# First loads of a gated two-branch mixer: their queues and order, a dummy gelu, and the count of products on zeros

## The chip, the cores and the metric

The kernel runs on one core of a Trainium2 chip. The metric is the device time of one execution in microseconds, as the median of several runs. A profile of one execution gives a span (from the first instruction of the program to its last) and that execution's own time, which is a little longer.

The engines are named as in the profile: PE (TensorE, matrix products; PEld its weight loads), DVE (VectorE), ACT (ScalarE), POOL (GpSimd) and SP (SyncE, which here only issues transfers). Transfers are issued by SP or by ACT, each on a queue of its own, and carried out by 16 DMA engines that both share.

## The reference

One sequence of 2048 tokens with 512 features goes through two branches, which a gate mixes. All tensors are bf16.

```python
x = A_x
g = _sigmoid((x * gate_w).sum(-1, keepdims=True))
a = _A_ref(x, A_wqkv, A_w_phi, A_wo)        # linear attention, 32 heads of 16
b = _B_ref(x, B_w_in, B_w_sp, B_b_sp, B_w_out)
return g * a + (1 - g) * b
```

Branch B is where the kernel starts:

```python
z = _gelu(jnp.einsum('bsd,df->bsf', x, w_in))    # w_in is 512 x 1376
z1 = z[..., :Fh].copy()
z2 = _layernorm(z[..., Fh:], axis=-1)
g = jnp.einsum('ts,bsf->btf', w_sp, z2) + b_sp[None, :, None]   # w_sp is 2048 x 2048
return jnp.einsum('bsf,fd->bsd', z1 * g, w_out)
```

Branch A projects x to q, k and v, applies a small matrix per head and a softmax of both signs to q and k, sums k times v over the sequence, and divides.

## The kernel before

The 2048 tokens are cut into 16 tiles of 128. The order of the instructions on each engine is written out by hand. The work goes in stages: z for every tile (with the projection of v and the folding of the heads' small matrix into the weights of q and k mixed in), then k's features beside the product with w_sp, then q's features, the rest of that product and the output tiles.

The change touches the opening alone. The names in it:

- `xn` (lines 109 and 112) holds the first two tiles of x as they lie in memory. `x_transpose(t)` (line 186) multiplies each with the identity matrix on PE, four products of 128x128, and two casts on DVE (line 195) write the result to `xT`, the transposed x that all projections read. The columns of `xT` for the other tiles come from transposing loads on SP (lines 116 and 122).
- `w_in` holds the weights of z in four blocks of 128 rows. It is loaded in pieces: columns 0 to 511 in two halves of two row blocks each (lines 110 and 111), columns 512 to 1023 (line 113) and columns 1024 to 1375 (line 115). Its last column, number 1376, is not loaded: `gate_column()` (line 197) puts gate_w there, so that the gate's sum comes out with z.
- `gw` (line 114) is gate_w as four rows, 1 KB.
- `z_piece(t, n0, n1)` (line 170) is four products (one per row block) for one tile and one of three column pieces, on line 173; `z_gelu` (line 203) is the gelu on ACT that reads the result. `z_post` (line 208) also writes `gth`, the tanh of the gate's sum, one column per tile.
- `spin(n)` (line 180) is n products of 128x128 on `warm`, a tile of zeros, whose result nobody reads.

The opening on PE runs in the order of lines 452 to 466: products on zeros, the transposition of tile 0, two more on zeros, the first piece of z for tile 0, the transposition of tile 1, the gate column, three on zeros, then the other pieces of z for tiles 0 and 1. Each step waits for the loads and casts that it reads. The cast into the gate column (line 201) waits for both halves of the first piece of w_in and for the third piece.

The issues of SP and ACT stand in lines 109 to 151; on SP each goes out when the one before it is done issuing. ACT loads its table for gelu ahead of the first gelu. Each later load on SP, from line 117 on, also waits for a load eight places earlier in the order of issue.

Of the kernel before, what the change touches and what calls it, by code (L numbers as in the profile page):

```python
# [7 lines left out]
AF = mybir.ActivationFunctionType  # L8
# [6 lines left out]
P = 128  # L15
# [4 lines left out]
F = 1376  # L20
# [4 lines left out]
CH = 512  # L25
# [14 lines left out]
def kernel(  # L40
# [14 lines left out]
    nc = tc.nc  # L55
    x2 = A_x.flatten_outer_dims()
# [10 lines left out]
    def zbank(t):  # L67
# [4 lines left out]
    w_in = pers.tile([P, NDT, F + 1], BF16, name="w_in")  # L72
# [16 lines left out]
    xn = pers.tile([P, 2, D], BF16, name="xn")  # L89
    warm = pers.tile([P, P], BF16, name="warm")  # L90
# [4 lines left out]
    gth = st[:, 1, :]  # L95
# [4 lines left out]
    gw = pers.tile([NDT, P], BF16, name="gw")  # L100
# [3 lines left out]
        out=ident[:], in_=ident[:], pattern=[[-1, P]],  # L104
# [2 lines left out]

    w_in_v = B_w_in.rearrange("(dt p) f -> p dt f", p=P)
    nc.sync.dma_start(out=xn[:, 0, :], in_=x2[0:P, :])
    nc.scalar.dma_start(out=w_in[:, 0:2, 0:CH], in_=w_in_v[:, 0:2, 0:CH])  # L110
    nc.sync.dma_start(out=w_in[:, 2:4, 0:CH], in_=w_in_v[:, 2:4, 0:CH])
    nc.scalar.dma_start(out=xn[:, 1, :], in_=x2[P:2 * P, :])
    nc.sync.dma_start(out=w_in[:, :, CH:2 * CH], in_=w_in_v[:, :, CH:2 * CH])
    nc.scalar.dma_start(out=gw[:], in_=gate_w.rearrange("(dt p) -> dt p", p=P))
    nc.sync.dma_start(out=w_in[:, :, 2 * CH:F], in_=w_in_v[:, :, 2 * CH:F])
    nc.sync.dma_start_transpose(out=xT[:, :, 2 * P:CH], in_=x2[2 * P:CH, :])
    nc.sync.dma_start(
        out=wv[:, :, :],
        in_=A_wqkv[:, 2 * D:3 * D].rearrange("(dt p) n -> p dt n", p=P),
    )  # L120
    for q in range(1, NCH):
        nc.sync.dma_start_transpose(
            out=xT[:, :, q * CH:(q + 1) * CH], in_=x2[q * CH:(q + 1) * CH, :]
        )
        if q == 1:
            nc.sync.dma_start(
                out=wphiW[:, :, :],
                in_=A_w_phi.rearrange("(g h) e f -> (h e) g f", g=NDT),
# [3 lines left out]
        out=bcolb[:, :, :], in_=B_b_sp.rearrange("(t p) -> t p", p=P)  # L132
# [7 lines left out]
    for t in range(WSLOTS):  # L140
        load_wsp(t)
    nc.sync.dma_start(
        out=w_out[:, 0:NFT - 1, :],
        in_=B_w_out[0:(NFT - 1) * P, :].rearrange("(ft p) n -> p ft n", p=P),
# [4 lines left out]
        out=w_out[0:last_m, NFT - 1, :], in_=B_w_out[(NFT - 1) * P:FH, :]  # L149
    )  # L150
    nc.sync.dma_start(
        out=wo[:, :, :], in_=A_wo.rearrange("(g p) n -> p g n", p=P)
# [4 lines left out]
        out=mask16[:], in_=mask16[:], pattern=[[-16, 8]],  # L157
# [3 lines left out]
        out=mask16[:], in_=mask16[:], pattern=[[16, 8]],  # L161
# [18 lines left out]
    def spin(n):  # L180
        for _ in range(n):
            nc.tensor.matmul(  # L182
                ps[:, 5, 0:P], lhsT=warm[:, 0:P], rhs=warm[:, 0:P], start=True, stop=True
            )

    def x_transpose(t):
        for dt in range(NDT):
            nc.tensor.matmul(
                ps[:, 6 + t, dt * P:(dt + 1) * P], lhsT=xn[:, t, dt * P:(dt + 1) * P],
                rhs=ident[:], start=True, stop=True,  # L190
            )
        src = ps[:, 6 + t, :].rearrange("p (d n) -> p d n", d=NDT)
        cols = slice(t * P, (t + 1) * P)
        for d in range(0, NDT, 2):
            nc.vector.tensor_copy(out=xT[:, d:d + 2, cols], in_=src[:, d:d + 2, :])  # L195
# [253 lines left out]
    oTpool = ctx.enter_context(tc.tile_pool(name="oTp", bufs=LAG + 2))  # L449

    VLAG = 5
    spin(24)
    x_transpose(0)
    spin(2)
    z_piece(0, *Z_PIECES[0])
# [104 lines left out]
```

## Time and profile before

| what | time, us |
|---|---|
| median of three runs | 210.62 |
| the three runs | 210.56, 210.62, 211.26 |
| the profiled execution, its own time | 210.52 |
| its span | 208.7 |
| PE busy in the span | 201.3 |
| first product on PE starts | 1.05 |
| first product of z starts | 4.74 |
| second run of products of z starts | 6.52 |
| bytes read from memory | 3.44 MB |

A row of the order of time gives the start and the length in microseconds, the engine (with a q where it is the engine's queue that issues a transfer), the line of the kernel, the operation, what is written and read, how many instructions were merged into the row, and in brackets the idle time before it and what ended it. A row of transfer issues gives the bytes of one and the time from issue to landing.

### The profile page before, as it was taken

What the parts mean: (1) busy time and instruction counts of PE and PEld (TensorE: products, weight loads), DVE (VectorE), ACT (ScalarE), POOL (GpSimd) and SP (SyncE); (2) the same over time, 40 slices, a digit from 0 to 9 for tenths busy, and PEclk for the clock granted to TensorE, in tenths of its full rate; (3) what the DMA queues carried; (4) which work ended last, traced back from release to release, by engine and by line L of the source; (5) the groups of instructions that cost most, each with busy time, mean ns of one, the idle gap of its engine ahead of it and who ended that gap; (6) DMA issues with size and microseconds to landing.
All of it is one profiled execution on the core that took longest, in us unless ns stands there. A gap on an engine that the chain in (4) does not pass through costs nothing.

```text
span 208.7 us, 3635 instructions
## 1 busy us (share of the span) xinstructions
PE 201.3 (96%) x1368; PEld 117.7 (56%) x1392; DVE 149.6 (72%) x306; ACT 81.4 (39%) x141; POOL 49.5 (24%) x46
## 2 busy tenths in 40 slices
PE   7999999999999999999999988999999999999994
PEld 6545455554456666666656655666454555555543
DVE  1367758295969888888884998877989688795500
ACT  2366766766684232424241420222424243241122
POOL 4000000000002535252522554211532243322000
PEclk9999999999999999999999999999999999999999
DMA  6999899994000653485358624756665775587431
GB/s 204 293 209 201 181 185 209 164 255 126 0 3 0 138 120 73 107 122 120 71 115 111 138 50 105 99 113 81 140 140 121 143 142 111 134 135 163 102 103 50
DMA packets 89818, 26.50 MB, mean 127 GB/s; under 512 B 84120, under 2 KB 89800, under 8 KB 89800
## 3 DMA queue, kind: packets, MB, share of 16 engines
q1 hardware_dynamic: 87072, 23.84, 58.3%
q10 hardware_dynamic: 2728, 2.43, 3.7%
q8 instruction: 11, 0.18, 0.4%
q14 instruction: 7, 0.06, 0.1%
HBM read 3.44 MB, written 2.10 MB: 27 GB/s over the span
## 4 chain that ended last, share of the span: by engine, by line
PE 90%; DVE 6%; issue 2%; ACT 0%; DVEq 0%
PE ps L385 31%; PE ps L173 18%; PE ps L316 12%; PE ps L428 10%; PE ps L271 7%; PE ps L433 7%; DVE zs L327 3%; PE ps L409 2%; PE ps L361 1%; DVE rs L329 1%; PE ps L182 1%; DVE u L393 1%; PE ps L294 1%; DVE xT L195 0%; DVE w_in L331 0%
## 5 line engine op out<-in xcount | busy, mean ns | idle before, releaser
L385 PE MATMUL ps<-zz,wsp 128*128 128x344 bf16 x512 | 79.4, 309 | 1.7 <-DVE u L393 1.6
L331 POOL TENSOR_TENSOR w_in<-w_in,rs 128x512 bf16<-128x512 bf16 x29 | 42.8, 1476 | 134.8 <-DVE rs L329 112.7
L385 PEld LDWEIGHTS <-wsp 128*128 128x128 bf16 x512 | 50.1, 98 | 30.1 <-issue 1.9
L322 ACT ACTIVATE w_in<-ps 128x512 bf16<-128x512 f32 x58 | 31.3, 596 | 65.9 <-POOL w_in L331 30.9
L173 PE MATMUL ps<-w_in,xT 128*128 128x512 bf16 (+1 forms) x189 | 39.1, 357 | 0.6 <-DVE xT L195 0.3
L327 DVE TENSOR_REDUCE zs<-w_in 128x64 f32<-128x1024 bf16 x29 | 35.1, 1210 | 0.0
L393 DVE SCALAR_TENSOR_TENSOR u<-ps,bcol,zz 128x344 bf16<-128x344 f32 x32 | 18.4, 575 | 19.9 <-PE ps L385 19.8
L204 ACT ACTIVATE zz<-ps 128x1376 bf16<-128x1376 f32 (+2 forms) x18 | 21.4, 1190 | 20.0 <-PE ps L173 18.0
L173 PEld LDWEIGHTS <-xT 128*128 128x128 bf16 x192 | 18.2, 97 | 18.6 <-DVE xT L195 1.3
L213 DVE BATCH_NORM_STATS2 stats<-zz 128x6 f32<-128x344 bf16 x32 | 14.9, 508 | 13.3 <-ACT zz L204 13.3
L428 PE MATMUL ps<-w_out,uT 128*128 128x512 bf16 (+1 forms) x100 | 23.4, 366 | 0.2
L331 DVE TENSOR_TENSOR w_in<-w_in,rs 128x512 bf16<-128x512 bf16 x29 | 20.1, 693 | 1.0
L329 DVE RECIPROCAL rs<-zs 128x64 f32<-128x64 f32 x32 | 17.7, 553 | 3.5 <-DVE zs L327 0.5
L437 ACT ACTIVATE ob<-ps 128x512 bf16<-128x512 f32 (+1 forms) x17 | 9.7, 572 | 25.5 <-PE ps L433 22.9
L433 PE MATMUL ps<-wo,oT 128*128 128x512 bf16 (+1 forms) x67 | 16.4, 366 | 0.0
L316 PE MATMUL ps<-wk,xT 128*128 128x512 bf16 x57 | 15.7, 378 | 0.3
L316 PE MATMUL ps<-wq,xT 128*128 128x512 bf16 x56 | 15.6, 378 | 0.3
L271 PE MATMUL ps<-wv,xT 128*128 128x512 bf16 x61 | 15.5, 379 | 0.2
L316 PEld LDWEIGHTS <-xT 128*128 128x128 bf16 x128 | 10.7, 97 | 8.5
L428 PEld LDWEIGHTS <-uT 128*128 128x128 bf16 x102 | 9.7, 98 | 10.0
L415 DVE SCALAR_TENSOR_TENSOR o<-ps,st,rd 128x512 bf16<-128x512 f32 x16 | 12.0, 751 | 0.6
L433 PEld LDWEIGHTS <-oT 128*128 128x128 bf16 x68 | 6.7, 98 | 7.2
(55 smaller groups left out, 115.2 us busy)
## 6 DMA issues: line engine op xcount, KB each, us to landing
out_dram<-ob ACTq DMA_DIRECT2D x15, 128.0 KB, 2.1
w_out<-in_B_w_out_dram SPq DMA_DIRECT2D x1, 640.0 KB, 6.1
w_in<-in_B_w_in_dram SPq DMA_DIRECT2D x1, 512.0 KB, 5.0
wv<-in_A_wqkv_dram SPq DMA_DIRECT2D x1, 512.0 KB, 5.3
wo<-in_A_wo_dram SPq DMA_DIRECT2D x1, 512.0 KB, 6.3
w_in<-in_B_w_in_dram SPq DMA_DIRECT2D x1, 352.0 KB, 5.6
w_in<-in_B_w_in_dram ACTq DMA_DIRECT2D x1, 256.0 KB, 3.3
w_in<-in_B_w_in_dram SPq DMA_DIRECT2D x1, 256.0 KB, 3.9
```

The costliest lines, as they stand in the source:

```text
L173: nc.tensor.matmul(zb[:, n0:n1], lhsT=xT[:, dt, t * P:(t + 1) * P], rhs=w_in[:, dt, n0:n1], start=(dt == 0), stop=(dt == NDT - 1),)
L204: nc.scalar.activation(out=zz[:, t, n0:n1], in_=zbank(t)[:, n0:n1], func=AF.Gelu_apprx_tanh)
L271: nc.tensor.matmul(ps[:, b, :], lhsT=xT[:, dt, t * P:(t + 1) * P], rhs=wv[:, dt, :], start=(dt == 0), stop=(dt == NDT - 1),)
L316: nc.tensor.matmul(ps[:, b, :], lhsT=xT[:, dt, t * P:(t + 1) * P], rhs=w[:, dt, :], start=(dt == 0), stop=(dt == NDT - 1),)
L322: nc.scalar.activation(out=e[:, :, a, :], in_=src, func=AF.Exp, scale=sc)
L327: nc.vector.tensor_reduce(out=zs[:], in_=ev, axis=AX.X, op=ALU.add)
L329: nc.vector.reciprocal(out=rs[:], in_=zs[:])
L331: eng.tensor_tensor(out=ev[:, sl, :], in0=ev[:, sl, :], in1=rs[:, sl, None].to_broadcast([P, H, DH]), op=ALU.mult,)
L385: nc.tensor.matmul(ps[:, b, 0:HF], lhsT=wsp[:, tt % WSLOTS, s, :], rhs=zz[:, s, FH + h * HF:FH + (h + 1) * HF], start=(s == 0), stop=(s == ...
L393: nc.vector.scalar_tensor_tensor(out=u[:, h * HF:(h + 1) * HF], in0=ps[:, b, 0:HF], scalar=bcol[:, tt:tt + 1], in1=zz[:, tt, h * HF:(h + 1 ...
L428: nc.tensor.matmul(ps[:, b, n0:n1], lhsT=uT[:, ft, :], rhs=w_out[:, ft, n0:n1], start=(ft == 0), stop=False,)
L433: nc.tensor.matmul(ps[:, b, n0:n1], lhsT=oT[:, g, :], rhs=wo[:, g, n0:n1], start=False, stop=(g == NDT - 1),)
```

## The change

The loads of the first two tiles of x and of the first two pieces of w_in all go to SP's queue, in the order in which PE uses them. On ACT the load of gate_w comes first; a gelu of one column of zeros follows, which writes column 0 of `gth` (written again by `z_post(0)` with its value); the third piece of w_in is issued from ACT behind it. `spin(24)` becomes `spin(21)`.

```diff
     nc.sync.dma_start(out=xn[:, 0, :], in_=x2[0:P, :])
-    nc.scalar.dma_start(out=w_in[:, 0:2, 0:CH], in_=w_in_v[:, 0:2, 0:CH])
+    nc.scalar.dma_start(out=gw[:], in_=gate_w.rearrange("(dt p) -> dt p", p=P))
+    nc.scalar.activation(out=gth[:, 0:1], in_=warm[:, 0:1], func=AF.Gelu_apprx_tanh)
+    nc.sync.dma_start(out=w_in[:, 0:2, 0:CH], in_=w_in_v[:, 0:2, 0:CH])
     nc.sync.dma_start(out=w_in[:, 2:4, 0:CH], in_=w_in_v[:, 2:4, 0:CH])
-    nc.scalar.dma_start(out=xn[:, 1, :], in_=x2[P:2 * P, :])
+    nc.sync.dma_start(out=xn[:, 1, :], in_=x2[P:2 * P, :])
     nc.sync.dma_start(out=w_in[:, :, CH:2 * CH], in_=w_in_v[:, :, CH:2 * CH])
-    nc.scalar.dma_start(out=gw[:], in_=gate_w.rearrange("(dt p) -> dt p", p=P))
-    nc.sync.dma_start(out=w_in[:, :, 2 * CH:F], in_=w_in_v[:, :, 2 * CH:F])
+    nc.scalar.dma_start(out=w_in[:, :, 2 * CH:F], in_=w_in_v[:, :, 2 * CH:F])
     nc.sync.dma_start_transpose(out=xT[:, :, 2 * P:CH], in_=x2[2 * P:CH, :])
...
     VLAG = 5
-    spin(24)
+    spin(21)
     x_transpose(0)
     spin(2)
     z_piece(0, *Z_PIECES[0])
```

## The prediction

> **What bounds the kernel now.** I read the page first: its span, its engine rows and its chain of waits.
>
> ```profile
> span 208.7 us, 3635 instructions
> PE 201.3 (96%) x1368; PEld 117.7 (56%) x1392; DVE 149.6 (72%) x306; ACT 81.4 (39%) x141; POOL 49.5 (24%) x46
> PE 90%; DVE 6%; issue 2%; ACT 0%; DVEq 0%
> ```
>
> TensorE (PE) is busy 96% of the span and 90% of the chain that ends last; no DMA stands in the chain. So a change in the loads counts only where TensorE waits, which is in the first microseconds. The second view is therefore the order of time of PE alone, from the start; a row is start, length, line, tile, count and the idle time before it.
>
> ```profile
> 1.05 2.74 PE L182 MATMUL ps<-warm 128*128 128x128 bf16 x24 [1.05 <-DVE warm L101]
> 3.59 0.63 PE L188 MATMUL ps<-ident,xn 128*128 128x128 bf16 x4
> 4.01 0.42 PE L182 MATMUL ps<-warm 128*128 128x128 bf16 x2
> 4.74 1.04 PE L173 MATMUL ps<-w_in,xT 128*128 128x512 bf16 x4 [0.31 <-DVE xT L195]
> 5.62 0.39 PE L188 MATMUL ps<-ident,xn 128*128 128x128 bf16 x4
> 6.04 0.34 PE L182 MATMUL ps<-warm 128*128 128x128 bf16 x3
> 6.52 7.82 PE L173 MATMUL ps<-w_in,xT 128*128 128x512 bf16 x38
> ```
>
> From 6.52 the products of z follow each other; before that the path is 24 products on zeros, four that transpose x's first tile, the DVE cast of those, and the first four of z. The first 24 start (2.74 - 0.31)/23 = 106 ns apart (0.31 is one product's own length on line 182), the second four transposes, the same shape, (0.39 - 0.22)/3 = 58 ns apart. So TensorE runs at half speed for the first three microseconds, though the granted clock column says 1.00 there. The third view is the issues of SP and ACT in order of time, cut here to four rows, and the fourth the page's times from issue to landing.
>
> ```profile
> 0.80 0.40 SPq L109 DMA_DIRECT2D xn<-in_A_x_dram  x1
> ...
> 2.78 2.53 SPq L116 DMA_TRANSPOSE xT<-in_A_x_dram  x1
> ```
>
> ```profile
> 1.81 0.58 ACTq L114 DMA_DIRECT2D gw<-in_gate_w_dram  x1
> 2.43 1.28 ACT L204 ACT_TABLE_LOAD   x1 [2.43 <-issue]
> ```
>
> ```profile
> w_in<-in_B_w_in_dram SPq DMA_DIRECT2D x1, 512.0 KB, 5.0
> w_in<-in_B_w_in_dram SPq DMA_DIRECT2D x1, 352.0 KB, 5.6
> w_in<-in_B_w_in_dram ACTq DMA_DIRECT2D x1, 256.0 KB, 3.3
> w_in<-in_B_w_in_dram SPq DMA_DIRECT2D x1, 256.0 KB, 3.9
> xn<-in_A_x_dram SPq DMA_DIRECT2D x1, 128.0 KB, 2.7
> xn<-in_A_x_dram ACTq DMA_DIRECT2D x1, 128.0 KB, 4.0
> ```
>
> Added to their issues (SP 0.80, 1.26, 1.72, 2.23; ACT 0.80, 1.29) these land: x's first tile 3.5, the first half of w_in's first piece 4.1, its second half 5.2, x's second tile 5.3, the second piece 6.7, the third 7.8. I call them x0, w01, w23, x1, p2 and p3.
>
> **The change, part by part.** *Three products on zeros less.* 3 x 106 ns = 0.32 us. x0 lands at 3.5 and the 24 products leave the array free at 1.05 + 24 x 0.106 = 3.59, so with the loads as they are only 0.09 us of it could be had: the gain needs x0 earlier. Gain between 0.09 and 0.32.
>
> *x0 alone on its queue.* Before, w01 is issued in the same instant from ACT. The table of stretches gives the bytes moved: 55 GB/s from 1.5 to 2.0, then 172, 256, 375, 352, 368, 382, 381, 377, 349 and 305 in half microseconds up to 7.0, that is 27 thousand bytes at 2.0, 113 at 2.5, 241 at 3.0, 429 at 3.5, 605 at 4.0, 789 at 4.5, 980 at 5.0, 1359 at 6.0, 1533 at 6.5 and 1686 at 7.0. x0 is 131 thousand, which are through at 2.57 if all bytes are its own. For the time to landing the nearest row is the stores of out, as large (128 KB) and on a queue with less ahead: 2.1 us, so 0.80 + 2.1 = 2.9. The other end is the old 3.5. The transposes want it at 1.05 + 21 x 0.106 = 3.28; I take 2.9, since w01 no longer shares, and so the full 0.32.
>
> *Four loads in line behind it.* SP's issues are 0.46 to 0.55 apart (the starts above), so w01 goes at 1.26, w23 at 1.72, x1 at about 2.2, p2 at about 2.7, and the transposing load of xT that stood at 2.78 at about 3.2. By the sums of bytes w01 (393 thousand up to it) is through at 3.4, w23 (655) at 4.1, x1 (786) at 4.5. From last byte to landing the old p3 shows how much to add at most: its 1670 thousand are through at 6.95, and it lands at 7.8, 0.85. x0's 2.9 less 2.57 gives 0.35 at least. TensorE, 0.32 earlier, wants w01 at 4.42, w23 with the third product of z at 4.74 + 2 x 0.22 - 0.32 = 4.86, and x1 at 5.62 - 0.32 = 5.30. They land at 3.75 to 4.25, 4.5 to 5.0 and 4.85 to 5.35: in time at the near end, 0.14 late at the far one. I take the near end, because the far lag comes from a stretch in which transposing loads already share.
>
> *gw first on ACT.* 1 KB; its issue (0.58) ends at 1.38, it is wanted at 5.93. Nothing.
>
> *Dummy gelu, and p3 behind it.* The table load (1.28) moves from 2.43 to about 1.42, the gelu of 128x1 costs as the tanh of line 211, 0.17 us: ACT idles there, the first real gelu is at 5.82. Without that cover it would be 1.45 us. p3's issue comes then at 1.42 + 1.28 + 0.17 = 2.87 if the queue holds it back behind both, and at 1.4 if it doesn't; no row of before has a DMA behind a table load on ACT. I take 2.87, the ACTIVATE behind the other table load (59.38, 1.28 long) starting at 60.67, when it is over. Its first byte is then at about 2.87 + 1.1 = 4.0 (x0's first bytes move between 1.5 and 2.0, 0.7 to 1.2 behind their issue), just when w23 is through. From then on p2 and p3 share, 884 thousand bytes after x1's 786: both are done at 6.95, as in the profile before. p3, wanted with the ninth product of z after 6.52, at 8.2 - 0.32 = 7.9, has lost its lead of 0.4 and kept its time. p2 is wanted at 6.52 + 4 x 0.22 - 0.32 = 7.1; alone it would be through at 5.9 (1310 thousand) and land at 6.25 to 6.75, shared at 6.95 and land at 7.3 to 7.8. So this part costs between 0 and 0.7; I take 0.15, as p2 was issued first and has a start of some of its bytes.
>
> By the Trainium skill, page "DMA: Bandwidth & Descriptors", section "Issuing engines are not separate DMA queues", loads from several engines run on the same 16 DMA engines and interleave. The trace agrees: the DMA share is at its full 1.06 to 1.10 from 3.0 to 6.0 with both queues in use. By this rule the bytes of all six loads end at 6.95 whatever queue they take, and the order alone decides.
>
> *SP's later loads.* One more plain issue ahead of them, 0.45 us. xT's columns for tile 2 (landed 2.78 + 5.9 = 8.7 by the page's median) are wanted at 10.3 - 0.32; the transposed wqk, issued 11.12 and landing 8.0 later at 19.1, at 20.3 - 0.32. With 0.45 more both still come in time, with 0.8 and 0.4 to spare.
>
> **Sum.** -0.32 + 0.15 = -0.17 against the profiled execution: span 208.7, its time 210.52, 1.8 us around the span that nothing here touches. That gives 210.35. The three runs have a median of 210.62, 0.1 above the profile, with 211.26 as the highest; I forecast 210.4.
>
> **Rivals.** *1. The loads eat it all.* p2 late by 0.5 to 0.7, or p3 issued at 1.4: its 360 thousand bytes then run ahead of w23, whose 1015 thousand are through at 5.1 and land at 5.45 or later against 4.86, 0.6 late. Either way -0.32 + 0.6 = +0.3, 210.8 (210.6 to 211.0). For it: the equal sums of bytes. Against: every wanted time but p2's has slack at the near end.
>
> *2. The clock rises later; this is the side of slower.* The full speed comes between 4.12 (last product at 106 ns) and 4.74, after 3.1 to 3.7 us in which TensorE had work but for the wait of 0.5 us before 4.74. With 21 products the work stops at 1.05 + 27 x 0.106 = 3.9 and pauses until 4.42, so less work stands ahead of the same instant: 27 products instead of 30. If 27 are too few, half speed lasts until as long a run has passed again, 4.42 + 3.1 to 3.7 = 7.5 to 8.1, and that time does half its work: 1.55 to 1.85 lost, less the 0.32 and the casts' waits: +1.1 to +1.5, 211.6 to 212.0. It decides from a threshold between 27 and 30 products. For it: 21 products end earlier than the step in speed. Against: the step came in the very pause, so it did not need full work to its end.
>
> The Trainium skill, page "TensorE: Matmul & The Clock Gate", section "Part 1: The HAM clock gate (the "warmup" mystery)", has the clock released after a free-running window of about 3.4 us of activity, so that the point varies between runs. The step at 4.1 to 4.7 agrees; by the rule some runs would show this price before and after alike.
>
> *3. x0 doesn't come sooner* (3.5): only the 0.09 is had, and p2 is in time: 210.4 to 210.5.
>
> **Chances.** Forecast (210.1 to 210.5) 0.45; rival 3, whose time can't be told from it, 0.12; rival 1 0.22; rival 2 0.16; a gain past 0.5%, for which I find no mechanism (all of the half speed given back would be 0.9 us), 0.05. Below 0.5%, 1.05 us, a change can't be told from none here. So same is 0.45 + 0.12 + 0.22 = 0.79, of which I give 0.02 to slower for rival 1's tail: faster 0.05, same 0.77, slower 0.18. The range runs from 209.9 (all 0.32 and the profile's own level, with the runs' spread) to 211.4, which takes in rivals 1 and 3 and leaves most of rival 2 out.
>
> **What would show it.** The first transpose on PE at 3.28 with no idle time ahead of it; x0's landing at 2.1 to 2.5 after its issue; the first product of z at 4.4 and the second run of them from 6.2; p3's issue on ACT at 2.9, not 1.4; idle time on PE ahead of z's fifth product if p2 is late. Rival 2 would show as z's first products 0.43 apart instead of 0.22. The prediction is wrong if TensorE's dense run starts later than 6.5, or if it starts at 6.2 and the end doesn't move with it.

## The result, and the profile after

The changed kernel takes 212.99 us in the median of 12 runs (211.39 to 213.49), the kernel before 210.84 in the 12 runs beside it (210.56 to 211.35): 0.8% slower, ratio 1.0079 with a 95% interval of 1.0053 to 1.0104. The medians alone stand 1.0102 apart, because the changed kernel's times lie in two groups, five at 211.39 to 211.97 and seven at 212.96 to 213.49, with none between. The forecast was 210.4, the range ended at 211.4. An execution more than 1.5% above the fastest of its kernel is left out of every ratio here; that is one, h1's at 214.40.

The profiled execution is one of the lower group, 211.57. First its page: the span, the chain of waits by engine, and the same chain by line.

```profile
span 209.9 us, 3629 instructions
PE 88%; DVE 6%; DMA 2%; issue 2%; SPq 0%; ACT 0%; DVEq 0%
PE ps L386 31%; PE ps L174 18%; PE ps L317 12%; PE ps L429 10%; PE ps L272 7%; PE ps L434 6%; DVE zs L328 3%; DMA w_in<-in_B_w_in_dram 2%; PE ps L410 2%; PE ps L362 1%; DVE rs L330 1%; DVE u L394 1%; PE ps L295 1%; DVE w_in L332 0%; DVE xn L332 0%
```

A transfer now stands in the chain, the load of w_in, with 2% of the span; before there was none. Where it stands shows in the order of time of PE (lines are one higher than before).

```profile
1.05 2.42 PE L183 MATMUL ps<-warm 128*128 128x128 bf16 x21 [1.05 <-DVE warm L101]
3.26 0.63 PE L189 MATMUL ps<-ident,xn 128*128 128x128 bf16 x4
...
4.42 1.03 PE L174 MATMUL ps<-w_in,xT 128*128 128x512 bf16 x2 [0.31 <-DVE xT L196]
6.33 0.59 PE L174 MATMUL ps<-w_in,xT 128*128 128x512 bf16 x2 [0.88 <-DMA w_in<-in_B_w_in_dram]
6.77 0.40 PE L189 MATMUL ps<-ident,xn 128*128 128x128 bf16 x4
...
7.69 6.52 PE L174 MATMUL ps<-w_in,xT 128*128 128x512 bf16 x32
```

Up to 4.42 all is 0.32 us earlier than before. Then the third product of z, which reads w23, starts at 6.33. Before it started at 4.74 + 2 x 0.22 = 5.18, and 1.34 later came the second run of z, at 6.52. Now it is 1.36 from 6.33 to 7.69. So the opening is -0.32 + 1.47 + 0.02 = 1.17 us longer, and the span is 1.2 longer (209.9 against 208.7): the end moved with the opening, and nothing was lost or won behind it. The two products at 4.42 take 1.03 together, the two at 6.33 take 0.59: the first two ran at half speed, which lies inside the wait.

Why w23 came late is in ACT's order of time, and in the times to landing:

```profile
0.80 0.56 ACTq L110 DMA_DIRECT2D gw<-in_gate_w_dram  x1
1.39 1.28 ACT L111 ACT_TABLE_LOAD   x1 [1.39 <-PEq L545]
1.45 0.41 ACTq L116 DMA_DIRECT2D w_in<-in_B_w_in_dram  x1
2.68 0.20 ACT L111 ACTIVATE st<-warm 128x1 f32<-128x1 bf16 x1
```

```profile
w_in<-in_B_w_in_dram SPq DMA_DIRECT2D x1, 512.0 KB, 5.4
w_in<-in_B_w_in_dram ACTq DMA_DIRECT2D x1, 352.0 KB, 5.0
```

ACT's queue (ACTq) issues p3 at 1.45, while the engine loads its table: neither the load nor the gelu behind it holds the issue back. So p3 goes out ahead of w23 (SP, 1.72), its 352 KB share the DMA engines with it, and it lands at 1.45 + 5.0 = 6.4, 1.5 before the cast that needs it starts (7.9), while w23 lands at about 6.3. p2, issued at 2.73, lands at 8.1.

### The profile page after: what moved, and what is told of

It is laid out like the page before. It is cut to its first block, busy times and chain, and to the rows that moved or that the text cites. A ratio compares the mean times of both kernels' runs of the same rounds, so it can differ in the third digit from the quotient of the medians.

```text
span 209.9 us, 3629 instructions
## 1 busy us (share of the span) xinstructions
PE 201.6 (96%) x1365; PEld 117.3 (56%) x1389; DVE 149.5 (71%) x306; ACT 81.6 (39%) x142; POOL 49.5 (24%) x46
## 4 chain that ended last, share of the span: by engine, by line
PE 88%; DVE 6%; DMA 2%; issue 2%; SPq 0%; ACT 0%; DVEq 0%
PE ps L386 31%; PE ps L174 18%; PE ps L317 12%; PE ps L429 10%; PE ps L272 7%; PE ps L434 6%; DVE zs L328 3%; DMA w_in<-in_B_w_in_dram 2%; PE ps L410 2%; PE ps L362 1%; DVE rs L330 1%; DVE u L394 1%; PE ps L295 1%; DVE w_in L332 0%; DVE xn L332 0%
```

## The experiments

The theories: **A**, p3's early issue makes w23 late; **B**, 21 products are too few for the clock; **C**, only the sum of the bytes counts; later **K**, the upper group of times is the clock, which the wait for w23 brings down; **D** and **E**, what is issued when, and on which queue, sets how fast the loads come. Each kernel ran beside the kernel before on the same chip; kernels of one table block shared a chip.

| kernel | median (range), us | ratio to before, 95% interval |
|---|---|---|
| e1: p3 truly waits for the gelu | 211.95 (211.57 to 212.22) | 1.0053, 1.0037 to 1.0068 |
| e2: p3 on SP behind p2 | 211.64 (211.27 to 212.03) | 1.0040, 1.0025 to 1.0055 |
| e3: the change, 24 products | 211.82 (211.57 to 213.68) | 1.0072, 1.0045 to 1.0098 |
| e4: before, p3 ahead of w23 | 212.64 (211.53 to 213.96) | 1.0081, 1.0049 to 1.0114 |
| | | |
| f1: the change, wait filled | 211.69 (211.38 to 212.07) | 1.0034, 1.0021 to 1.0048 |
| f2: e2, w01 and w23 as one load | 211.77 (210.87 to 212.80) | 1.0042, 1.0020 to 1.0065 |
| f3: before, gw first, 21 products | 212.17 (211.34 to 213.32) | 1.0060, 1.0034 to 1.0086 |
| f4: before, 21 products | 211.23 (210.69 to 211.50) | 1.0011, 0.9998 to 1.0023 |
| | | |
| g1: e2, w01 on ACT at 0.80 | 211.61 (211.13 to 212.63) | 1.0034, 1.0019 to 1.0049 |
| g2: before, w01 on SP | 211.69 (211.12 to 213.23) | 1.0039, 1.0020 to 1.0058 |
| g3: the change again | 213.34 (213.22 to 213.45) | 1.0108, 1.0087 to 1.0129 |
| g4: e4, wait filled | 212.04 (211.75 to 212.25) | 1.0047, 1.0028 to 1.0065 |
| | | |
| h1: before, x1 on SP | 211.78 (211.10 to 214.40) | 1.0037, 1.0021 to 1.0052 |
| h2: before, first cast's wait filled | 210.95 (210.57 to 211.48) | 0.9998, 0.9984 to 1.0013 |

### Is it p3's place? (e1, e2, e3, e4)

e1, against the change:

```diff
-    nc.scalar.activation(out=gth[:, 0:1], in_=warm[:, 0:1], func=AF.Gelu_apprx_tanh)
+    nc.scalar.activation(out=w_in[:, 3, F - 1:F], in_=warm[:, 0:1], func=AF.Gelu_apprx_tanh)
```

> The changed kernel, with the dummy gelu writing the last loaded column of w_in's third piece (p3 overwrites it), so that p3's load truly waits for the gelu. Theory A (p3's 360 thousand bytes, issued at 1.45, go ahead of the second half of w_in's first piece, w23, and TensorE waits for that): p3 is issued at 2.9 instead of 1.45, w23 lands by 4.9 instead of 6.3, the second run of z's products starts at 6.2 to 6.5 instead of 7.7, time 210.3 to 210.8. Theory B (21 products are too few for the clock, the loads are secondary): w23 lands earlier all the same, but z's first products stay 0.43 us apart and the time stays at 211.5 or above. Theory C (all the loads share the DMA engines, only the sum of bytes counts): w23 lands after 5.8, time as the change's.

e2, against the change:

```diff
-    nc.scalar.dma_start(out=w_in[:, :, 2 * CH:F], in_=w_in_v[:, :, 2 * CH:F])
+    nc.sync.dma_start(out=w_in[:, :, 2 * CH:F], in_=w_in_v[:, :, 2 * CH:F])
```

> The changed kernel with p3's load back on SP's queue, behind w_in's second piece, everything else as changed. Theory A: w23 lands by 4.9, z's second run of products starts at 6.2 to 6.5, time 210.3 to 210.8; p3 lands near 7.8 and is wanted at 7.9, so at most 0.2 us of wait there. Theory B: 211.5 or above. Theory C: as the change.

In e1 p3 is issued at 2.91, and w23 no longer holds up z's third product. The order of time of PE in e1 from there on:

```profile
4.42 1.52 PE L174 MATMUL ps<-w_in,xT 128*128 128x512 bf16 x4 [0.31 <-DVE xT L196]
6.22 0.40 PE L189 MATMUL ps<-ident,xn 128*128 128x128 bf16 x4 [0.27 <-DMA xn<-in_A_x_dram]
...
7.13 1.04 PE L174 MATMUL ps<-w_in,xT 128*128 128x512 bf16 x4
8.57 0.59 PE L174 MATMUL ps<-w_in,xT 128*128 128x512 bf16 x2 [0.40 <-DMA w_in<-in_B_w_in_dram]
```

The four products follow each other, but the next two waits have moved up: x1 at 6.22, p2 at 8.57 (wanted at 7.1 + 4 x 0.22 = 8.0). In e2 the four products take longer:

```profile
4.42 1.89 PE L174 MATMUL ps<-w_in,xT 128*128 128x512 bf16 x4 [0.31 <-DVE xT L196]
```

They run at half speed, and TensorE does not stand still for x1, which lands at 2.23 + 3.8 = 6.0, just before they end. z's second run starts at 7.08, p2 comes at 8.40, and the cast that waits for p3 costs 0.35 us more. So A holds for w23, and C falls. B does not fall here: half speed in z's first products and a median above 211.5 are what it expected; e3 and f4 decide on it. A's time (210.3 to 210.8) is missed by about 1 us in both: undoing p3's early issue gives back 0.3 to 0.4% of the 0.8%, and the rest has another cause. The upper group is absent in both (six runs each).

e3, against the change, and e4, against the kernel before:

```diff
-    spin(21)
+    spin(24)
```

```diff
+    nc.sync.dma_start(out=w_in[:, :, 2 * CH:F], in_=w_in_v[:, :, 2 * CH:F])
     nc.sync.dma_start(out=w_in[:, 2:4, 0:CH], in_=w_in_v[:, 2:4, 0:CH])
...
-    nc.sync.dma_start(out=w_in[:, :, 2 * CH:F], in_=w_in_v[:, :, 2 * CH:F])
```

> The changed kernel with 24 products on zeros instead of 21. Theory A: w23 still lands near 6.3, so the three products cost nothing or little; z's second run starts at 7.4 to 7.7; time within 0.3 of the change's. Theory B: the clock has risen by z's first products (0.22 apart), and the time falls by 0.4 to 1.5 us toward 211 or below, without the slower of the two groups into which the change's times fall (211.4 to 212.0 and 213.0 to 213.5).

> The kernel before with one load moved: p3 is issued on SP ahead of w23, at 1.26, all else as before (24 products, two queues). Theory A: w23 lands about 1 us later than its 5.1 (360 thousand bytes at 370 GB/s), TensorE waits 0.8 to 1.1 us inside the first piece of z, time 211.5 to 212.0 or more. Theory B: 24 products keep the clock, the time stays within 0.4 of before's. Theory C: no change, 210.6 to 210.9.

24 products change neither group (five runs at 211.57 to 211.97, three at 212.90 to 213.68), and z's first two products still take 0.94 us together in its profile: B falls as the cause of the groups. e4 makes the loss of the change, both groups included (four runs at 211.53 to 212.00, four at 213.28 to 213.96), out of the kernel before by moving p3 ahead of w23 and nothing else: in its profile z's third product waits 1.65 us (0.8 to 1.1 expected) and starts at 7.07. So p3's place, not its queue, suffices for the wait.

### What is the upper group? (f1, g3, g4)

f1 and g4 put 10 and 15 products on zeros between the second and third product of z (f1 against the change, g4 against e4 with 15 for 10):

```diff
                 start=(dt == 0), stop=(dt == NDT - 1),
             )
+            if t == 0 and n0 == 0 and dt == 1:
+                spin(10)
```

> The changed kernel with ten more products on zeros between the second and third product of z's first piece, where TensorE waits for w23 (5.3 to 6.3 in the profile of the change). Theory K (the slower group of the change's times, 213.0 to 213.5, comes of the clock: the wait leaves too little work in the window by which the clock is raised or kept): w23 lands as before, near 6.3, all the runs come out at 211.2 to 212.1 and none at 213, though ten products are added. Rival (the slower group comes of the loads, landing later in some executions): both groups stay, 211.4 to 212.0 and 213.0 to 213.5, or all are later by up to 0.5.

> The change itself once more, for its two groups of times on the chip of the next run. Theory K (clock): both groups again, near 211.4 to 212.0 and 213.0 to 213.5; if the profile is of the slower group, its products of z stand 0.43 apart for about 3.4 us longer than in the other, with the loads landing as in the other (w23 at 6.1 to 6.8). Rival (loads): in the slower group w23 lands a microsecond or more later than 6.5.

> The kernel before with p3 issued ahead of w23 (e4), and fifteen more products on zeros in the wait for w23 (5.4 to 7.1 in e4). Theory K: e4's slower group (213.3 to 214.0, four runs of eight), in whose profile the granted clock fell back to 0.50 from 8.3 to 11.8, is gone: all runs at 211.4 to 212.2. Rival (loads): the slower group stays, or the fifteen products add up to 0.5 to all.

All five runs of the change on g3's chip are of the upper group, where both groups were expected, and so is its profile. Three rows of PE's order of time, and the table by stretches (PE, PEld, DVE, ACT and POOL busy with counts, then granted clock, DMA share, GB/s):

```profile
4.42 0.61 PE L174 MATMUL ps<-w_in,xT 128*128 128x512 bf16 x2 [0.30 <-DVE xT L196]
6.72 0.59 PE L174 MATMUL ps<-w_in,xT 128*128 128x512 bf16 x2 [1.70 <-DMA w_in<-in_B_w_in_dram]
...
8.06 5.12 PE L174 MATMUL ps<-w_in,xT 128*128 128x512 bf16 x18
```

```profile
7.00:8.00 1.00, 1.00 (x10) 0.57 (x8) 0.42 (x2) 0.60 (x1) 0.00 (x0) 0.81 1.65 256
8.00:9.00 1.00, 1.00 (x4) 0.39 (x4) 0.41 (x3) 0.00 (x0) 0.00 (x0) 0.50 0.90 222
9.00:10.00 1.00, 1.00 (x4) 0.34 (x3) 0.00 (x0) 0.00 (x0) 0.00 (x0) 0.50 1.11 313
10.00:11.00 1.00, 1.00 (x3) 0.30 (x2) 0.00 (x0) 0.00 (x0) 0.00 (x0) 0.50 1.19 304
11.00:12.00 1.00, 1.00 (x7) 0.59 (x6) 0.00 (x0) 0.55 (x1) 0.00 (x0) 0.98 1.27 290
```

The loads are those of the other profile to 0.4 us: w23 ends the wait at 6.72 instead of 6.33, z's second run starts at 8.06 instead of 7.69. But here the clock was up early (z's two products took 0.61, not 1.03), TensorE then stood still for 1.70, and from 7.6 to 11.0 the granted clock is 0.50. A mean of 0.81 from 7 to 8 is 0.62 of it at full and 0.38 at half speed, so it fell at 7.6; the 3.0 us of z from 8.06 at half speed cost 1.5. With 0.37 from the loads this makes the 1.8 by which the span (211.7) exceeds the other (209.9). So K holds for this profile, and the rival, later loads, falls for the larger part.

How far this reaches is told by the mean granted clock over the span, which is on record for every execution. 3.4 us at 0.50 make it 0.992. That is what four of these five have, but only one of the seven upper runs in the section on the result; the other six have 1.000. A clock that is late from the start leaves no mark in that figure: f2's and f3's profiled executions (212.20 and 212.56) have 0.999 and yet take 1.86 us for z's first four products, where the kernel before takes 1.04. Whether the six lost their time that way isn't shown.

The wait filled, the upper group is gone: none of six runs in f1 (on a chip on which the change itself did not run), none of six in g4, on the chip on which all five of the change were in it. g4 was expected at 211.4 to 212.2 and ends at 212.25, f1 at 211.2 to 212.1; the added products cost nothing that shows. The Trainium skill, page "TensorE: Matmul & The Clock Gate", section "Part 1: The HAM clock gate (the "warmup" mystery)", has a window of about 3.4 us, which runs freely, decide on the clock; the stretch of 3.4 us here agrees.

### What is left when p3 is put right? (f2, f3, f4, g1, g2, h1)

f4 is the kernel before with `spin(21)`; f3 besides issues gw ahead of w01 on ACT:

```diff
+    nc.scalar.dma_start(out=gw[:], in_=gate_w.rearrange("(dt p) -> dt p", p=P))
     nc.scalar.dma_start(out=w_in[:, 0:2, 0:CH], in_=w_in_v[:, 0:2, 0:CH])
...
-    nc.scalar.dma_start(out=gw[:], in_=gate_w.rearrange("(dt p) -> dt p", p=P))
...
-    spin(24)
+    spin(21)
```

> The kernel before with 21 products on zeros instead of 24 and nothing else. Loads as before: x0 lands at 3.5, so the transposes start 0.09 earlier at most. Theory (the count of products matters only through x0): 210.4 to 210.9. Theory B (the clock needs the 24): first products of z 0.43 apart, 211.3 to 212.

> The kernel before with two edits only: on ACT, gw's load goes ahead of w01 (so that x0 has the DMA engines to itself), and 21 products on zeros. All other loads keep the two queues of before. Theory (two queues keep the DMA engines supplied, x0 is all that had to come sooner): x0 lands at 2.9 to 3.1, w01 by 4.5, w23 by 5.2, x1 by 5.6, p2 by 6.9; z's first product at 4.4, its second run at 6.2 to 6.5, time 210.3 to 210.8 with the clock as before. Rival (21 products are too few for the clock): first products of z 0.43 apart, a group of runs at 211.3 or above.

f4 can't be told from before (1.0011, 0.9998 to 1.0023), and six of its ten runs are below 211.3, where B's range begins; its transposes start at 3.53, so without an earlier x0 the 21 products are worth 0.06. f3 gets x0 early (first transpose at 3.27) and loses it: w01, issued 0.6 later than before, is awaited until 5.51, 1.39 us of idle time, and z's first four products then run at half speed, ratio 1.0060. The stretch in which this happens, in the kernel before and then in the change:

```profile
2.50:3.00 0.50, 0.50 (x8) 0.50 (x6) 0.09 (x1) 0.50 (x1) 0.48 (x3) 1.00 0.85 256
```

```profile
2.50:3.00 0.50, 0.50 (x8) 0.50 (x6) 0.09 (x1) 0.38 (x2) 0.48 (x3) 1.00 0.74 96
```

With nothing large issued beside x0 at 0.80, x0's bytes are through at about 2.5 and the next have hardly begun: 96 GB/s instead of 256 (80 in f3, 152 in e2). Up to 5.0 the change has moved 811 thousand bytes, the kernel before 980. The gap alone does not rank the kernels: g1, which has w01 beside x0 again, has moved 153 thousand up to 3.0 and the change 193, yet g1 is ahead at 5.0 with 878.

f2 loads w_in's first piece on SP in one issue; g1 is e2 with w01 back on ACT as its first issue; g2 is the kernel before with w01 on SP. The three edits:

```diff
-    nc.sync.dma_start(out=w_in[:, 0:2, 0:CH], in_=w_in_v[:, 0:2, 0:CH])
-    nc.sync.dma_start(out=w_in[:, 2:4, 0:CH], in_=w_in_v[:, 2:4, 0:CH])
+    nc.sync.dma_start(out=w_in[:, :, 0:CH], in_=w_in_v[:, :, 0:CH])
```

```diff
+    nc.scalar.dma_start(out=w_in[:, 0:2, 0:CH], in_=w_in_v[:, 0:2, 0:CH])
     nc.scalar.dma_start(out=gw[:], in_=gate_w.rearrange("(dt p) -> dt p", p=P))
...
-    nc.sync.dma_start(out=w_in[:, 0:2, 0:CH], in_=w_in_v[:, 0:2, 0:CH])
```

```diff
-    nc.scalar.dma_start(out=w_in[:, 0:2, 0:CH], in_=w_in_v[:, 0:2, 0:CH])
+    nc.sync.dma_start(out=w_in[:, 0:2, 0:CH], in_=w_in_v[:, 0:2, 0:CH])
```

> The kernel with all loads on SP (e2), and w_in's first piece as one load of 512 KB instead of two of 256 KB: one issue less, so x1 is issued at 1.8 instead of 2.2, the second piece (p2) at 2.3 instead of 2.7. Theory D (on one queue the loads are limited by the spacing of their issues, 0.46 to 0.5 us each, and the DMA engines run half empty between 4.5 and 5.5): x1 lands at 5.3 to 5.7 instead of 6.0, p2 at 7.6 to 8.0 instead of 8.4, the stretch 4.5 to 5.5 moves more than 250 GB/s instead of 185. Rival (one queue is slower whatever the issues, or the memory sets the rate): x1 and p2 land within 0.2 of e2's times. Time 211.0 to 211.6 by D, as e2 (211.3 to 212.0) by the rival.

> The kernel with all loads on SP (e2), and the first half of w_in's first piece (w01) back on ACT, as its first issue at 0.80; 21 products and the dummy gelu stay. Theory D (what is issued beside x0 at 0.80 keeps the DMA engines supplied; without it they run half empty from 2.5 to 3.0 and all later loads land later): the stretch 2.5 to 3.0 moves more than 200 GB/s instead of 152 (e2) or 96 (the change), the sum of bytes up to 5.0 is 900 thousand or more instead of 811 to 833, x0 lands at 3.4 to 3.5 again and w23 by 5.3; time 210.6 to 211.3, near the kernel before with 21 products (210.7 to 211.5). Rival (x1 on SP, one issue more ahead of the second and third piece, is what costs): bytes and time as e2 (211.3 to 212.0).

> The kernel before with w01 alone moved from ACT to SP, behind x0; x1 and gw stay on ACT, x1 now issued at 0.80; 24 products. Theory D: x1 fills the DMA engines beside x0, so the stretch 2.5 to 3.0 moves more than 200 GB/s; x1 lands by 4.2, w01 by 4.7, w23 by 5.4, the second piece one issue later, by 7.3 to 8.2; time 210.6 to 211.3. Rival (SP's queue alone is slow to feed w_in's loads): 2.5 to 3.0 below 160 GB/s, w23 after 5.6, time 211.3 or above.

f2 shows D's landings (x1 3.9 after an issue at 1.73, p2 at 7.1 and so earlier than expected, 375 to 381 GB/s from 4.5 to 5.5), but z's first product now waits for the whole piece, until 5.29, and half of its runs are in an upper group (212.20 to 212.80, five of ten). g1 shows D's bytes from 2.5 to 3.0 (221 GB/s), but 878 thousand instead of 900 up to 5.0, and p2 lands at 8.2. Its time is the rival's, but in its profile the cause is not: TensorE does not wait for p2, and z's first piece runs at half speed.

```profile
4.72 1.89 PE L174 MATMUL ps<-w_in,xT 128*128 128x512 bf16 x4 [0.31 <-DVE xT L196]
7.56 5.78 PE L174 MATMUL ps<-w_in,xT 128*128 128x512 bf16 x27
```

From 4.72 to 7.56 is 2.84 us, where the kernel before takes 1.78 (4.74 to 6.52), and x1 had landed at 5.3. So about 1.1 of the 1.3 us by which the span (210.0) is longer is the clock. g2 moves what D expected too, 334 GB/s from 2.5 to 3.0, yet w01 lands at 5.2 and w23 at 5.9, later than D has it, and the time is the rival's. D explains the gap at 2.5 and not the rest; the three have in common with e1 and e2 that p2 stands further back on SP, by one issue (2.2 to 2.3 us) and in e1 and e2 by two (2.7).

h1 makes only that move in the kernel before:

```diff
-    nc.scalar.dma_start(out=xn[:, 1, :], in_=x2[P:2 * P, :])
+    nc.sync.dma_start(out=xn[:, 1, :], in_=x2[P:2 * P, :])
```

> The kernel before with x1's load alone moved from ACT to SP, behind w23, so that w_in's second piece (p2) and third (p3) are issued at 2.2 and 2.7 instead of 1.7 and 2.2. Theory E (the issue slot on SP is what is left): x0, w01 and w23 land as before (3.5, 4.2, 5.1), p2 at 7.8 to 8.4 and p3 at 8.8 to 9.4, time 211.0 to 211.6, ratio 1.001 to 1.003. Rival (p2 and p3 vary by a microsecond between executions anyway, the slot is nothing): 210.5 to 211.2 and a ratio within 0.001 of 1.

The order of time of PE in h1, and its table by stretches:

```profile
6.52 1.04 PE L173 MATMUL ps<-w_in,xT 128*128 128x512 bf16 x4
8.20 1.02 PE L173 MATMUL ps<-w_in,xT 128*128 128x512 bf16 x4 [0.63 <-DMA w_in<-in_B_w_in_dram]
9.58 3.74 PE L173 MATMUL ps<-w_in,xT 128*128 128x353 bf16 x19 [0.36 <-DVE w_in L201]
```

```profile
4.50:5.00 0.50, 0.26 (x2) 0.11 (x2) 0.50 (x2) 0.00 (x0) 0.00 (x0) 1.00 1.16 262
5.00:5.50 0.50, 0.50 (x4) 0.29 (x3) 0.02 (x1) 0.00 (x0) 0.00 (x0) 1.00 0.61 152
```

Up to 6.52 it is the kernel before, each row within 0.01 us. Then TensorE waits 0.63 for p2 and 0.36 for the cast that needs p3, and the ratio is 1.0037 (1.0021 to 1.0052), as much as e2 or g1 lose. The products behind the two waits start 0.8 and 1.3 later than before (8.20 against 7.40, 9.58 against 8.26), which is the whole of the 1.3 by which the span (210.0) is longer. E holds, and its time and ratio were expected too small; that the same slot is what is left in g1 does not follow, since there the profile has the clock. p2, issued 0.5 later (2.23), lands at 2.23 + 5.9 = 8.1 instead of 6.7. The DMA engines move 262 and 152 GB/s from 4.5 to 5.5, where the kernel before moves 382 and 381. Why they run short there isn't settled: a load of 128 KB takes up an issue of the same length on SP as one of 512 KB, which fits, but f4 has the loads of the kernel before and its p2 took 6.0 to land (at 7.7; in h2 at 6.9), so p2 also varies from one execution to the next.

### Does the kernel before gain by filling a wait? (h2)

```diff
     x_transpose(0)
-    spin(2)
+    spin(6)
```

> The kernel before with six products on zeros instead of two behind the first transposes, so that TensorE works through its wait of 0.5 us for the first cast. Theory K: in the executions in which the clock rises late it rises sooner; the upper half of before's times (210.8 to 211.5) moves down, median 0.1 to 0.4 below before's, ratio 0.998 to 0.9995. Rival (the spread is that of the loads): ratio within 0.001 of 1, or 0.1 us above where the four products are not hidden.

0.9998 (0.9984 to 1.0013): no difference. The spread of the kernel before isn't made in that wait. f4's profiled execution, 211.38, shows another place, with the loads of before: z's second run starts 0.25 later than in the profile before (6.77), and the product behind the cast that needs p3 0.96 later (9.22 against 8.26), so that late p2 and p3 make about 0.7 of it. No version that ran is faster than the kernel before.

## Why the prediction was wrong

**The gain was right.** 3 x 106 ns and x0 at 2.9: the first transpose came at 3.26 (3.28 forecast), z's first product at 4.42 (4.4).

**The step that failed** is the one on p3: "I take 2.87", on the ground that an ACTIVATE behind the other table load had waited for it. That row shows the engine waiting; p3 is issued by ACT's queue, which here did not wait for its engine, and went out at 1.45. The prediction had named that end (1.4), and made it part of rival 1.

**A second step failed with it,** the landings in "Four loads in line behind it" and of p2. With p3 held back (e1), w23 lands at 4.9, as reckoned (4.5 to 5.0), but x1 at 2.23 + 3.9 = 6.1 instead of 4.85 to 5.35, and p2 at 2.74 + 5.8 = 8.5 instead of 7.3 to 7.8; the time is still 1.0053. So the forecast would have failed without p3's early issue as well.

**Rival 1's price was too small.** It put w23 0.6 late for p3 at 1.4; it was 1.47. 1015 thousand bytes were to be through at 5.1, by the bytes per stretch of the kernel before. In the change 990 thousand are through at 5.5 and 1172 at 6.0, so 1015 at 5.6; and w23 landed 0.7 behind that, where 0.35 was reckoned (the bounds were 0.35 to 0.85). The sums carried over a rate that belongs to the old issues, two of them at 0.80: moving w01 to 1.26 left the engines at 96 GB/s from 2.5 to 3.0, and at 5.0 there were 811 thousand bytes through instead of 980.

**Rival 2 had the clock and its price right, but not its cause.** It made the count of 21 products decide; f4 and e3 show that it doesn't by itself. What brings the upper group is the stop for w23: filled (f1, g4), the group is gone. Which executions it strikes isn't shown; in the two profiles of the change the stop is 0.9 and 1.7 us, with the clock late in the first and early in the second. So rival 2's 1.5 us comes on top of rival 1's in some executions, and the prediction, which took the rivals as alternatives, ended its range at 211.4, below both groups but for one run. The sign that it gave for rival 2, z's first products 0.43 apart, also shows outside that group: e2, f2, f3 and g1, all with 21 products, take 1.86 to 1.89 us for the first four, h1 with 24 takes 1.04. But f4 with 21 takes 1.37, and no run separates the count from the waits there; this stays open.

**x1's move was priced as one issue slot** whose cost to p2 was taken at 0.15 of a possible 0.7. Alone (h1) it costs 0.37%, 0.63 us at p2 and 0.36 at the cast behind p3.

**The Trainium skill's rule** on page "DMA: Bandwidth & Descriptors", section "Issuing engines are not separate DMA queues", by which several issuing engines save no more than issue time, isn't what h1's profile shows: the same load at the same place of the program, moved from ACT to SP, costs p2 1.4 us where the issue is 0.5. One profile does not settle it, since with the loads unmoved p2 lands at 6.7, 6.9 and 7.7 (before, h2, f4). What the prediction drew from the rule did fail: the 1670 thousand bytes of the six loads were to be through at 6.95 on whatever queue, and by the same count they are at 7.4 in the change and at 7.9 in h1.

**Right was** that the later loads on SP would have room: nothing after the opening differs, and the end moved with it.

## What to carry to other kernels

Where one engine is busy to the end, a load that is early by itself can make another late: a transfer put on a second queue to get out of the way must be held by a dependency, since here a table load and an activation ahead of it on that engine did not hold it (issued at 1.45, with a dependency at 2.91). Sums of bytes from the old profile hold only for the old issue times. A stop of TensorE in its first microseconds is to be priced twice, once as idle time and once as the half-speed stretch that it may bring.

## What was not expected of the hardware

A load on ACT's queue was issued 0.06 us after the start of a table load of 1.28 on the same engine. The granted clock rose and then fell back to 0.50 for 3.4 us after a stop of 1.70 us, in the middle of otherwise dense work. And a granted clock of 1.00 in the first stretches can't be taken at its word: in f2's profile the column says 1.00 while z's first four products take 1.86 us instead of 1.04.
